# Decode attention and MLP on one core: two row blocks of one head group's query weights per layer, laid on 56 partitions and loaded from GpSimd

## The chip, the cores and the metric

The kernel runs on one core of one Trainium2 chip. The metric is the device time of one execution in microseconds. Three executions of the kernel before took 1343.22, 1343.85 and 1345.13 us; the median is 1343.85 us.

## The reference

One token of width 640 passes through attention, an MLP, the same attention again and the same MLP again, each with a residual:

```
def _A_ref(x, k_cache, v_cache, wq, wo):
    q = (x @ wq).reshape(B, Sq, H, Dh).transpose(...)
    scores = einsum("bhqd,bhkd->bhqk", q, k_cache) * (Dh ** -0.5)
    o = einsum("bhqk,bhkd->bhqd", softmax(scores), v_cache)
    return o.transpose(...).reshape(B, Sq, H * Dh) @ wo
x = x + _A_ref(_layernorm(x), k_cache, v_cache, wq, wo)
x = x + relu(_layernorm(x) @ w1) @ w2
x = x + _A_ref(_layernorm(x), k_cache, v_cache, wq, wo)
x = x + relu(_layernorm(x) @ w1) @ w2
```

There are 32 heads of width 128 and 8192 cached positions, all in float32. The keys and values of one head are 8.4 MB, and both layers read the same cache, so each layer streams some 268 MB from HBM; a few units are kept on chip between the layers. The query weights `wq` are 640 x 4096, the output weights `wo` 4096 x 640.

## The kernel before, in words

**The stream.** The host lays keys and values out as units of up to 6 MB, each with 128 rows, one for each SBUF partition. `pump` (line 179) issues the next unit on SyncE's DMA queue as soon as `place` (line 160) finds room for it in one large tile, `ring`; `release` (line 248) frees a piece when the matmuls that read it have been written out, and calls `pump` again. The tail of the same tile, `by_parts`, holds blocks of `w2`, and at the start of layer 1 two units of keys and values.

**The heads.** For each head `scores` (line 511) multiplies the keys by the query, `largest`, `exponentials` and `turn` make the probabilities, `values` (line 562) multiplies the values by them, `output` (line 582) adds the parts up. The order of the heads is fixed by `HEADS`; four heads make a group, eight groups a layer.

**The weights of a group.** The tile `both_t` has 5120 floats for each partition. Its first half, `wq_t`, holds the query weights of one group: five row blocks ("chunks", 128 rows of `wq` each) of 512 columns, one row of a block on each partition. The second half, `wo_t`, holds the output weights of a group. `load_wo` (line 276) fills both halves with a single load from the array `wqo`, in which the query weights of group k+1 lie beside the output weights of group k; it is issued on ScalarE's DMA queue (line 280, 2560 KB).

**The order of the side work.** `due` (line 778) appends small tasks to two lists, `chores` and `slow`, when a head begins, and `side_work` (line 804) takes a step of them between the pieces of a head. `run_out(k)` (line 725) multiplies the outputs of group k by `wo` and then calls `load_wo(L, k + 1, ...)`; it is due at the first head of group k+1. `queries_of(k + 1)` is due at the third head of group k; its `wide_queries` (line 435) makes the queries of a whole group by five matmuls, one for each chunk, whose partial sums lie in four strips of one PSUM bank (lines 440 and 452 to 459):

```
for c in range(NB):
    strip = c % 4
    nc.tensor.matmul(pq[32 * strip : 32 * strip + 32],
                     xc[:, c : c + 1].to_broadcast([P, 32]), wq_t[:, c], ...)
```

**GpSimd** has almost nothing to do in the kernel before: a few memsets at the start and one power (line 336, `inv_std`) for each layer norm. It issues no DMA.

Of the kernel before, what the change touches and what calls it, by code (L numbers as in the profile page):

```python
# [10 lines left out]
F32 = mybir.dt.float32  # L11
# [4 lines left out]
P = 128  # L16
D = 640
H = 32
SK = 8192
DH = 128  # L20
DFF = 1728
EPS = 1e-5
NB = D // P
HG = 4
NG = H // HG
# [58 lines left out]
GROUPS = [[heads[a] // HG for a in range(0, H, HG)] for heads in HEADS]  # L84
# [3 lines left out]
RING = 4248  # L88
WC_AT = [5, 8]
MIX_AT = [[7, 9, 11, 13], [12, 16, 20, 24]]  # L90
FLAT = 3072
EDGE = 4096
BIG = 1536
# [19 lines left out]
W2_UNITS = SLOTS * D // 8  # L113
# [10 lines left out]


@with_exitstack
def decode_kernel(ctx: ExitStack, tc: tile.TileContext, x, kv, wq, wo, wqo, w1, w2, out):
    nc = tc.nc
    consts = ctx.enter_context(tc.tile_pool(name="consts", bufs=1))
    wts = ctx.enter_context(tc.tile_pool(name="wts", bufs=1))  # L130
# [7 lines left out]

    ring = consts.tile([P, 8 * (RING + W2_UNITS)], F32, name="ring")
    by_parts = ring[:, 8 * RING :]
# [8 lines left out]
    dram_at, o = {}, 0  # L151
# [119 lines left out]
    wo_t = both_t[:, HG * D :].rearrange("p (j d) -> p j d", d=D)  # L271

    def load_wq(g, queue):
        queue.dma_start(both_t[:, : HG * D], wq[P * g : P * g + P])

    def load_wo(L, k, queue):

        g = GROUPS[L][k]
        if 0 < k < NG - 1:
            queue.dma_start(both_t, wqo[L, k - 1])  # L280
# [132 lines left out]
    def queries(g, xc, r):  # L413

        pq = side
        for c in range(NB):
            for j in range(HG):
                nc.tensor.matmul(
                    pq[32 * j : 32 * j + 32, :DH],
                    xc[:, c : c + 1].to_broadcast([P, 32]),  # L420
                    wq_t[:, c, j * DH : (j + 1) * DH],
                    start=(c == 0),
                    stop=(c == NB - 1),
                )
        yield "dve"
        row = work.tile([P, DR], F32, name="q_row")[:, :DH]
        nc.vector.tensor_scalar(row, pq[:, :DH], r[0], SCALE, op0=ALU.mult, op1=ALU.mult)
        yield "pe"
        pt = side
        nc.tensor.matmul(pt[:, :HG], row, sel[:, :HG], start=True, stop=True)  # L430
        yield "dve"
        qT[g] = work.tile([P, HG], F32, name="qT", bufs=2)
        nc.vector.tensor_copy(qT[g], pt[:, :HG])

    def wide_queries(g, xc, r):

        pq = side
        for c in range(NB):
            strip = c % 4
            nc.tensor.matmul(  # L440
                pq[32 * strip : 32 * strip + 32],
                xc[:, c : c + 1].to_broadcast([P, 32]),
                wq_t[:, c],
                start=c < 4,
                stop=c in (1, 2, 3, 4),
                skip_group_check=True,
            )
# [246 lines left out]
    def attention_and_mlp(L, xr, s, before=None):  # L694
# [25 lines left out]
                    queue.pop(0)  # L720

        def queries_of(k):
            yield from wide_queries(groups[k], xc, r)

        def run_out(k):

# [51 lines left out]
        def due(h):  # L778

            where = heads.index(h)  # L780
            k, j = divmod(where, HG)
            if j == 0:
                o_cols[k] = work.tile([P, HG], F32, name="o_cols", bufs=2)
                sums[k] = work.tile([P, HG], F32, name="sums", bufs=2) if k < NG - 1 else None
            if where and j == 0:
                chores.append([run_out(k - 1), "pe"])
            if j == 2 and k + 1 < NG:
                slow.append([queries_of(k + 1), "pe"])
            if where == H - 2:
                chores.append([first_of_last(), "pe"])  # L790
            if where == H - 1:
                chores.append([before_last(), "pe"])
            if L == 0 and where == H - HG:
                slow.append([centre_query(NG - 1, HG - 1), "pe"])
            if L == 0 and where == 4:
                nc.scalar.dma_start(w1_t, w1)
            if where == WC_AT[L]:
                nc.scalar.dma_start(wo_last, wo[last // HG][:, last % HG])
# [85 lines left out]
    def mlp(L, o, last, xp, ph):  # L884
# [128 lines left out]
        for c in range(NB):  # L1013
            g = c % 4
            nc.tensor.matmul(
                pq[32 * g : 32 * g + 32, :DH],
                cols[:, c : c + 1].to_broadcast([P, 32]),
                wq_t[:, c, (HG - 1) * DH :],
                start=c < 4,
                stop=c in (1, 2, 3, 4),  # L1020
                skip_group_check=True,
            )
# [43 lines left out]
def _laid_out(A_x, A_k_cache, A_v_cache, A_wq, A_wo, B_w1, B_w2):  # L1066
    k = np.asarray(A_k_cache)[0].reshape(H, 4, 4, RUN, DH).transpose(0, 4, 1, 2, 3)
    v = np.asarray(A_v_cache)[0].reshape(H, 4, 4, NBL, 4, 32, DH).transpose(0, 1, 5, 3, 4, 2, 6)
    v = v.reshape(H, P, NBL, 4, 4, DH)
    kv = np.empty(H * P * SK * 2, k.dtype)  # L1070
    o = 0
    for u in ORDER:
        n = 8 * size(u)
        block = kv[o : o + P * n].reshape(P, n)
        o += P * n
        a = 0
        for h, kind, piece in UNITS[u[0]][u[1]]:
# [12 lines left out]
    w2[W2_LAST:, -1, : D // 2] = w2[:W2_LAST, -1, D // 2 :]  # L1090
    wq = np.asarray(A_wq).reshape(NB, P, NG, HG * DH).transpose(2, 1, 0, 3).reshape(NG, P, HG * D)
# [5 lines left out]
    return {  # L1097
        "x": np.repeat(np.asarray(A_x).reshape(D)[_COLS].reshape(4, DR), 32, axis=0),
        "kv": kv,
        "wq": wq.reshape(NG * P, HG * D),  # L1100
        "wo": wo,
        "wqo": np.array(wqo),
        "w1": np.asarray(B_w1).reshape(NB, P, DFF).transpose(1, 0, 2),
        "w2": np.array(
            [
                np.concatenate(
                    [
                        np.concatenate([w2[:, b, : w2_width((b,))] for b in part], 1).reshape(-1)
                        for part in loads
                    ]  # L1110
                )
                for loads in W2_LOADS
            ]
        ),
    }


# [22 lines left out]
```

## Time and profile before

| | |
|---|---|
| median of three executions | 1343.85 us |
| profiled execution, span from its first to its last instruction | 1340.6 us |
| its own time: the span and what lies around it | not given apart; the median is 3.25 us above the span |
| HBM read | 570.83 MB, 426 GB/s over the span |
| busy: TensorE matmul, VectorE, ScalarE, GpSimd | 65%, 22%, 5%, 0% |
| DMA, mean busy share of 16 engines | 9 tenths or more in 39 of 40 slices |

The page gives the busy time of each engine, the span in forty slices, the DMA queues, the chain of work that ended last, the costliest groups of instructions and the DMA issues. q1 is the queue that SyncE fills, q10 that of ScalarE, q8 and q14 carry instructions. The "DMA share" of a window is the time that the packets begun in it took, as a share of 16 engines' time; 9/16 is 0.56.

### The profile page before, as it was taken

Reading aid. Unit: us, or ns where it says so; the run is one execution under the profiler, and the core shown is the slowest. Engines: PE = TensorE matmul, PEld = TensorE weight load, DVE = VectorE, ACT = ScalarE, POOL = GpSimd, SP = SyncE. Lnnn points to the kernel's source line nnn. Section 1 sums busy time; section 2 is a strip of 40 time slices with the busy share of each in tenths; the row PEclk is TensorE's granted clock in tenths of the full one; section 3 lists DMA queues with packets and bytes.
Section 4 is the critical chain, followed back from the end, with each engine's and each line's share of the span. In section 5 each row is a group of like instructions: output and inputs, shape, how many; then the busy total and the mean of one; then the engine's idle time right before and its main releaser. Section 6 shows DMA issues by size and latency. Waiting matters only on the chain.

```text
span 1340.6 us, 13403 instructions
## 1 busy us (share of the span) xinstructions
PE 874.0 (65%) x5806; PEld 255.5 (19%) x5806; DVE 290.2 (22%) x956; ACT 62.6 (5%) x155; POOL 2.9 (0%) x10
## 2 busy tenths in 40 slices
PE   5463575767657656676688755657566666567687
PEld 2110121111111111112243211112111111111123
DVE  2120121211212112223123212221221212212222
ACT  0000000000000000000000000000000000000000
POOL 0000000000000000000000000000000000000000
PEclk8686787988777887788799977887778787888789
DMA  9999999999999999999999999999999999999998
GB/s 395 431 435 430 442 423 437 429 428 437 432 434 429 428 439 426 433 425 415 425 396 425 430 435 433 432 433 431 433 429 434 432 428 433 437 427 436 425 424 333
DMA packets 24546, 571.70 MB, mean 426 GB/s; under 512 B 2724, under 2 KB 2984, under 8 KB 6952
## 3 DMA queue, kind: packets, MB, share of 16 engines
q1 hardware_dynamic: 21464, 529.31, 92.1%
q10 hardware_dynamic: 3024, 41.53, 7.3%
q8 instruction: 46, 0.75, 0.2%
q14 instruction: 12, 0.10, 0.0%
HBM read 570.83 MB, written 0.00 MB: 426 GB/s over the span
## 4 chain that ended last, share of the span: by engine, by line
DMA 67%; PE 27%; DVE 4%; ACT 1%; issue 1%; SPq 0%; ACTq 0%; DVEq 0%
DMA ring<-in_kv 66%; PE ps L516 10%; PE outs L570 9%; PE side L672 1%; DMA ring<-in_w 1%; DVE p L591 1%; PE acc L621 1%; PE side L440 1%; ACT p L545 1%; DVE h_t L531 1%; PE small L536 1%; PE small L604 1%; PE side L454 1%; DVE p L552 0%; DVE h_t L537 0%
## 5 line engine op out<-in xcount | busy, mean ns | idle before, releaser
L516 PE MATMUL ps<-ring,spread_q 128*32 128x512 f32 (+3 forms) x2088 | 332.7, 727 | 149.2 <-DMA ring<-in_kv 148.6
L570 PE MATMUL outs<-ring,p 128*4 128x512 f32 (+3 forms) x2080 | 310.6, 732 | 164.1 <-DMA ring<-in_kv 95.7
L531 DVE TENSOR_REDUCE h_t<-ps 128x1 f32<-128x512 f32 x64 | 44.3, 691 | 365.4 <-PE ps L516 365.4
L570 PEld LDWEIGHTS outs<-ring,p 128*4 128x4 f32 x2080 | 50.6, 95 | 348.4 <-issue 233.8
L516 PEld LDWEIGHTS ps<-ring,spread_q 128*32 128x32 f32 x2088 | 63.9, 124 | 277.5 <-issue 188.8
L545 ACT ACTIVATE p<-ps,h_t 128x512 f32<-128x512 f32 x63 | 43.3, 687 | 1161.2 <-DVE h_t L537 1161.2
L552 DVE STREAM_TRANSPOSE p<-p 128x128 f32<-128x128 f32 x256 | 79.8, 312 | 63.9 <-ACT p L545 57.2
L587 DVE TENSOR_SCALAR p<-outs,ind 128x128 f32<-128x128 f32 x64 | 22.5, 351 | 317.2 <-PE outs L570 317.2
L604 PE MATMUL small<-ones,p 128*128 128x1 f32 (+1 forms) x128 | 25.3, 267 | 97.4 <-DVE p L591 97.4
L591 DVE SCALAR_TENSOR_TENSOR p<-outs,ind,p 128x128 f32<-128x128 f32 x188 | 66.0, 351 | 6.7
L536 PE MATMUL small<-ident,h_t 128*128 128x128 f32 x128 | 32.7, 339 | 40.1 <-DVE h_t L531 39.9
L604 PEld LDWEIGHTS small<-ones,p 128*128 128x128 f32 x128 | 19.9, 195 | 159.7 <-DVE p L591 158.9
L672 PE MATMUL side<-w_t,wct 128*128 128x448 f32 (+1 forms) x80 | 45.3, 651 | 0.0
L452 DVE TENSOR_SCALAR q_row<-side,ln_r 128x128 f32<-128x128 f32 x56 | 19.5, 349 | 106.0 <-PE ps L516 59.0
L440 PE MATMUL side<-both_t,ln_xc 128*32 128x512 f32 x140 | 37.3, 844 | 0.0
L536 PEld LDWEIGHTS small<-ident,h_t 128*128 128x128 f32 x128 | 20.0, 196 | 89.0 <-DVE h_t L531 85.5
L621 PE MATMUL acc<-both_t,o_cols 128*64 128x320 f32 x220 | 34.6, 458 | 0.0
L454 PEld LDWEIGHTS side<-sel,q_row 128*128 128x128 f32 x112 | 19.3, 216 | 56.3 <-DVE q_row L452 29.9
L537 DVE TENSOR_REDUCE h_t<-small 128x1 f32<-128x128 f32 x64 | 18.7, 292 | 35.4 <-PE small L536 35.4
L454 PE MATMUL side<-sel,q_row 128*128 128x1 f32 x112 | 24.1, 284 | 0.3 <-DVE q_row L452 0.2
L621 PEld LDWEIGHTS acc<-both_t,o_cols 128*64 128x64 f32 x220 | 15.5, 147 | 29.4 <-issue 17.7
L672 PEld LDWEIGHTS side<-w_t,wct 128*128 128x128 f32 x80 | 13.5, 211 | 32.4 <-issue 32.4
(148 smaller groups left out, 219.5 us busy)
## 6 DMA issues: line engine op xcount, KB each, us to landing
ring<-in_kv SPq DMA_DIRECT2D x50, 6144.0 KB, 35.0
ring<-in_kv SPq DMA_DIRECT2D x23, 4096.0 KB, 33.2
ring<-in_kv SPq DMA_DIRECT2D x29, 2048.0 KB, 27.7
both_t<-in_wqo ACTq DMA_DIRECT2D x12, 2560.0 KB, 24.7
ring<-in_kv SPq DMA_DIRECT2D x4, 5120.0 KB, 34.6
ring<-in_kv SPq DMA_DIRECT2D x9, 1024.0 KB, 23.9
w_t<-in_w ACTq DMA_DIRECT2D x1, 4320.0 KB
ring<-in_kv SPq DMA_DIRECT2D x5, 768.0 KB, 29.5
```

The source lines that it names most:

```text
L440: nc.tensor.matmul(pq[32 * strip : 32 * strip + 32], xc[:, c : c + 1].to_broadcast([P, 32]), wq_t[:, c], start=c < 4, stop=c in (1, 2, 3, ...
L454: nc.tensor.matmul(mine[:, :1], row, one_of_each, start=True, stop=True, skip_group_check=True)
L516: nc.tensor.matmul(hd.ps[32 * g : 32 * g + 32, c : c + n], spread_q[:, 3 - r : 35 - r], tile_of[:, at + g * n : at + (g + 1) * n], start=f ...
L531: nc.vector.tensor_reduce(hd.nm, hd.ps, AX.X, ALU.max, negate=True)
L536: nc.tensor.matmul(pt[:, :P], hd.nm.to_broadcast([P, P]), ident, start=True, stop=True)
L545: nc.scalar.activation(hd.p, hd.ps, AF.Exp, bias=hd.low, scale=scale, accum_out=hd.l)
L552: nc.vector.transpose(hd.all_p[:, b * P : (b + 1) * P], hd.p[:, b * P : (b + 1) * P])
L570: nc.tensor.matmul((hd.out if r0 < 2 else hd.out_2)[32 * g : 32 * g + 4, r0:r1].rearrange("p r d -> p (r d)"), hd.all_p[:, 32 * i : 32 * i ...
L591: nc.vector.scalar_tensor_tensor(oc, hd.out[:, r], ind[:, r : r + 1], oc, op0=ALU.mult, op1=ALU.add)
L604: nc.tensor.matmul(pt[:, :n], part, mask.to_broadcast([P, n]), start=i == 0, stop=i == len(parts) - 1,)
L621: nc.tensor.matmul(acc[64 * g : 64 * g + 64, : 2 * DR], col.to_broadcast([P, 64]), wt[:, 2 * DR * g : 2 * DR * (g + 1)], start=first, stop ...
L672: nc.tensor.matmul(pt[:, :n], wct[:, c], w1_t[:, c, f : f + n], start=(c == 0), stop=(c == NB - 1),)
```

## The change

For the load with k = 2 of each layer (the query weights of the fourth group in order) two of the five chunks, numbers 3 and 4, leave the load on ScalarE's queue. Their 256 rows of 512 floats are laid on 56 partitions instead of 128: 44 partitions hold five rows each, 12 hold three (`held`). GpSimd loads them with 15 DMAs (`loads`), from a new array `early` in HBM: nine carry data (partitions 0 to 11, 16 to 19, 28 to 31, 96 to 99 and 92 to 95, then 32 to 43 with three slots, 48 to 51, 60 to 67 and 124 to 127), and six carry four or twelve floats a partition that nothing reads. The first number of a load is how many pieces its source is divided into where that is more than one; a load with a 1 there has three or five pieces against four partitions. The rows of a partition lie in up to five slots of 512 + 8 floats; the slots take the first two chunks' place in `both_t` and 1576 floats before it, so `both_t` is now the last part of `ring`, with 1600 more floats in front of it that were unused and are set to zero at the start. `POS` puts chunks 4 and 3 first in `wq_t`, so that the rest is one stretch.

The matmul of such a slot needs the normalized input in the order in which the rows lie. `early_columns`, due at the fifth head of each layer, makes these columns: two matmuls bring the columns of chunks 3 and 4 into a row, eight copies of VectorE put their pieces in place on a zeroed row in `mix`, five small matmuls turn the row back into five columns. `wide_queries` then uses three whole chunks and five slots for that group: eight matmuls instead of five.

```
+EARLY = {2: dict(chunks=[3, 4], slots=5,
+        held=[(5, [(0, 12), (16, 4), (28, 4), (48, 4), (60, 8), (92, 8), (124, 4)]),
+              (3, [(32, 12)])],
+        loads=[(3, 0, 12, 5), (1, 12, 4, 0), (1, 16, 4, 5), (2, 20, 8, 0),
+               (1, 28, 4, 5), (1, 96, 4, 5), (6, 68, 24, 0), (1, 92, 4, 5),
+               (3, 32, 12, 3), (1, 12, 4, 0), (1, 48, 4, 5), (2, 20, 8, 0),
+               (2, 60, 8, 5), (6, 68, 24, 0), (1, 124, 4, 5)])}
+EARLY_IN = [[2], [2]]
...
+def split(load):
+    engines, _, rows, slots = load
+    pieces = engines if engines > 1 else slots or 3
+    n = rows * (slots * HG * DH if slots else 12 if engines == 1 else 4)
+    return pieces, n // pieces
...
-    both_t = wts.tile([P, 2 * HG * D], F32, name="both_t")
+    both_t = ring[:, both_at:]
...
+    def load_early(L, k):
+        spec = EARLY[k]
+        for i, load in enumerate(spec["loads"]):
+            engines, first, rows, slots = load
+            pieces, n = split(load)
+            o = EARLY_AT[L, k, i]
+            o_end = o + pieces * (n + GAP)
+            source = early[o:o_end].rearrange("(g m) -> g m", g=pieces)[:, :n]
+            where = slots_of(spec)[first : first + rows]
+            if slots:
+                where = where[:, :slots, : HG * DH]
...
+            nc.gpsimd.dma_start(where, source)
...
         if 0 < k < NG - 1:
-            queue.dma_start(both_t, wqo[L, k - 1])
+            n = HG * DH * len(EARLY[k]["chunks"]) if k in EARLY_IN[L] else 0
+            queue.dma_start(both_t[:, n:], wqo[L, k - 1, :, n:])
+            if k in EARLY_IN[L]:
+                load_early(L, k)
             return
...
+    nc.vector.memset(ring[:, both_at - 8 * 200 : both_at], 0.0)
...
+    def early_columns(L, xc):
+        for i, c in enumerate((3, 4)):
+            nc.tensor.matmul(pt[:32, i * P : (i + 1) * P],
+                xc[:, c : c + 1].to_broadcast([P, 32]), ident, start=True, stop=True)
+        yield "dve"
+        nc.vector.memset(row, 0.0)
...
+                nc.vector.tensor_copy(row[:, a : a + slots, first : first + m], source)
...
+        yield "pe"
+        for s in range(n):
+            nc.tensor.matmul(pt[:, s : s + 1], row[:, s], sel[:32, :1], start=True, stop=True)
+        yield "dve"
+        held = work.tile([P, 8], F32, name="early_x")
+        nc.vector.tensor_copy(held[:, :n], pt[:, :n])
...
-    def wide_queries(g, xc, r):
+    def wide_queries(g, xc, r, k=None):
...
+        parts = [(xc[:, c : c + 1], wq_t[:, POS[c]]) for c in range(NB)]
+        if k in early_x:
+            spec = EARLY[k]
+            parts = [p for c, p in enumerate(parts) if c not in spec["chunks"]]
+            parts += [(early_x[k][:, s : s + 1], slots_of(spec)[:, s, : HG * DH])
+                      for s in range(spec["slots"])]
...
+            if where == 4:
+                slow.append([early_columns(L, xc), "pe"])
```

More of the change, by code (lines that the diff above doesn't have):

```diff
@@ L90, with placed, filled @@
 MIX_AT = [[7, 9, 11, 13], [12, 16, 20, 24]]
+POS = {4: 0, 3: 1, 0: 2, 1: 3, 2: 4}
+SLOT = HG * DH + 8
+GAP = 64
+EARLY = {
+    2: dict(
+        chunks=[3, 4],
+        slots=5,
+        held=[
+            (5, [(0, 12), (16, 4), (28, 4), (48, 4), (60, 8), (92, 8), (124, 4)]),
+            (3, [(32, 12)]),
+        ],
+        loads=[
+            (3, 0, 12, 5),
+            (1, 12, 4, 0),
+            (1, 16, 4, 5),
+            (2, 20, 8, 0),
+            (1, 28, 4, 5),
+            (1, 96, 4, 5),
+            (6, 68, 24, 0),
+            (1, 92, 4, 5),
+            (3, 32, 12, 3),
+            (1, 12, 4, 0),
+            (1, 48, 4, 5),
+            (2, 20, 8, 0),
+            (2, 60, 8, 5),
+            (6, 68, 24, 0),
+            (1, 124, 4, 5),
+        ],
+    ),
+}
+EARLY_IN = [[2], [2]]
+def placed(spec):
+    o = 0
+    for slots, runs in spec["held"]:
+        n = sum(m for _, m in runs)
+        for first, m in runs:
+            yield slots, first, m, o, n
+            o += m
+        o += (slots - 1) * n
+def filled(spec):
+    at = np.full((spec["slots"], P), -1)
+    for slots, first, m, o, n in placed(spec):
+        for s in range(slots):
+            for i in range(m):
+                c, d = divmod(o + s * n + i, P)
+                at[s, first + i] = P * spec["chunks"][c] + d
+    held = np.sort(at[at >= 0])
+    assert (held == np.concatenate([P * c + np.arange(P) for c in spec["chunks"]])).all()
+    loaded = np.zeros((spec["slots"], P), bool)
+    for _, first, rows, slots in spec["loads"]:
+        loaded[:slots, first : first + rows] = True
+    assert loaded[at >= 0].all()
+    return at
+def split(load):
[3 more added lines that the diff above has]
+    return pieces, n // pieces
+EARLY_AT, _o = {}, 0
+for _L in range(2):
+    for _k in EARLY_IN[_L]:
+        for _i, _load in enumerate(EARLY[_k]["loads"]):
+            EARLY_AT[_L, _k, _i] = _o
+            _pieces, _n = split(_load)
+            _o += _pieces * (_n + GAP)
+EARLY_SIZE = _o
 FLAT = 3072
@@ L126, in decode_kernel @@
 @with_exitstack
-def decode_kernel(ctx: ExitStack, tc: tile.TileContext, x, kv, wq, wo, wqo, w1, w2, out):
+def decode_kernel(ctx: ExitStack, tc: tile.TileContext, x, kv, wq, wo, wqo, w1, w2, early, out):
     nc = tc.nc
     consts = ctx.enter_context(tc.tile_pool(name="consts", bufs=1))
-    wts = ctx.enter_context(tc.tile_pool(name="wts", bufs=1))
     work = ctx.enter_context(tc.tile_pool(name="work", bufs=1))
@@ L722, in queries_of @@
         def queries_of(k):
-            yield from wide_queries(groups[k], xc, r)
+            yield from wide_queries(groups[k], xc, r, k - 1)
         def run_out(k):
@@ L1114, in _laid_out @@
         ),
+        "early": early,
     }
```

71 lines of the change are left out of this document (62 added, 9 removed).

## The prediction

> **What bounds the kernel now.** I read the page's head and queues first, then windows of time, then the chain of waits around the two places where the stream ends.
>
> ```profile
> span 1340.6 us, 13403 instructions
> PE 874.0 (65%) x5806; PEld 255.5 (19%) x5806; DVE 290.2 (22%) x956; ACT 62.6 (5%) x155; POOL 2.9 (0%) x10
> DMA packets 24546, 571.70 MB, mean 426 GB/s; under 512 B 2724, under 2 KB 2984, under 8 KB 6952
> q1 hardware_dynamic: 21464, 529.31, 92.1%
> q10 hardware_dynamic: 3024, 41.53, 7.3%
> q8 instruction: 46, 0.75, 0.2%
> DMA 67%; PE 27%; DVE 4%; ACT 1%; issue 1%; SPq 0%; ACTq 0%; DVEq 0%
> ```
>
> The queues' shares add up to 99.6% of 16 engines' span: the DMA engines hardly ever rest, and what each of them has to carry sets the end. A row on q1 moves at 529.31 MB / (0.921 x 16 x 1340.6 us) = 26.8 KB per us and engine, one on q10 at 41.53 / (0.073 x 16 x 1340.6) = 26.5. So a row of keys and values of 49,152 bytes takes 1.83 us.
>
> The share of the engines that still have something to do, in windows before the two ends of the stream (columns: window, length, busy time of five engines, granted clock, DMA share, GB/s):
>
> ```profile
> 300.00:500.00 200.00, 125.41 (x724) 32.10 (x728) 39.83 (x127) 7.51 (x19) 0.00 (x0) 0.80 1.00 432
> 634.00:639.00 5.00, 2.39 (x52) 1.09 (x43) 0.00 (x0) 0.00 (x0) 0.00 (x0) 1.00 0.93 354
> 690.00:696.00 6.00, 5.23 (x91) 4.22 (x94) 1.55 (x7) 0.74 (x3) 0.00 (x0) 1.00 0.88 335
> 1300.00:1331.00 31.00, 25.57 (x256) 10.59 (x248) 8.96 (x31) 2.30 (x7) 0.00 (x0) 1.00 1.01 421
> 1331.00:1332.70 1.70, 1.44 (x41) 1.30 (x45) 0.17 (x1) 0.00 (x0) 0.00 (x0) 1.00 0.74 300
> 1332.70:1334.70 2.00, 1.99 (x54) 1.58 (x50) 0.68 (x4) 0.00 (x0) 0.00 (x0) 1.00 0.54 221
> 1334.70:1336.40 1.70, 1.51 (x34) 0.89 (x26) 0.49 (x4) 0.00 (x0) 0.55 (x1) 1.00 0.33 120
> ```
>
> All 16 engines work until 1331.0. From 1332.7 to 1334.7 the share is 0.54, close to 9/16 = 0.56; the last engine ends at about 1336.4. So seven engines finish some 4.5 us before the last, though every load gives each the same bytes. The idle time in the last three windows is (0.26 x 1.7 + 0.46 x 2.0 + 0.67 x 1.7) x 16 = 40 us of one engine: a perfect balance would end 2.5 us sooner. In layer 0 the seven run dry at 634 to 639 and 690 to 696 (5.6 and 11.5 us of one engine). What the nine have more is probably the instruction queue: 46 packets at 0.2% of 16 x 1340.6 us, some 43 us, or 4.8 us for each of nine engines over both layers. That is an inference; no row names an engine.
>
> ```profile
> 573.46 34.55 DMA ring<-in_kv
> 622.83 17.26 DMA ring<-in_kv
> 648.54 35.72 DMA ring<-in_kv
> 1316.50 19.15 DMA ring<-in_w
> 1335.70 0.75 PE side L482 x16
> ```
>
> The chain (start, length, what) runs over such landings, and a load has landed only when the last engine has. What the nine late engines are spared before 648 and before 1316 therefore comes off the end in both layers.
>
> **The change part by part.**
>
> *The load on ScalarE's queue.* Its rows shrink from 20,480 to 16,384 bytes in one load of each layer; with 128 rows on 16 engines each engine is spared 8 x 4,096 = 32,768 bytes, at 26.5 KB/us 1.24 us a layer, 2.47 us in all.
>
> *The nine data loads.* 512 KB come back on 56 partitions, eight partitions for each of seven engines: 40 rows of 2,048 bytes on four engines, 32 on three, that is 3.09 and 2.47 us, less the 1.24 spared: +1.85 and +1.23 us. The seven early engines have about 4.5 us at 1336 and take this without becoming last: in layer 1 they would end near 1331.9 + 1.85 = 1333.8, the nine at 1335.2. That the chosen seven are the early seven rests on the number alone.
>
> *Six idle loads and fifteen completion marks.* Every one of the 15 loads may leave a mark on all 16 engines, and the idle loads give the nine a few packets of 16 bytes. No row has their price. Below: nothing. Above: as much as the nearest row with a size, the 2,560-byte row of `wo_last` (0.097 us at 26.5), 15 times a layer, 1.45 us, which would eat the gain.
>
> ```profile
> q10 hardware_dynamic: 288, 2.95, 17.0%
> wo_last<-in_wo ACTq DMA_DIRECT2D x1, 320.0 KB, 36.5
> L798 ACTq DMA_DIRECT2D wo_last<-in_wo x2: 334/334/335, 127.2 to 823.9; - x2
> ```
>
> In the 41 us from 124 to 165 q10's 288 packets, marks among them, took 0.17 x 16 x 41 = 111.5 us of one engine, and 2.95 MB at 26.5 are 111.3: small packets cost next to nothing beyond their bytes. I take 0.02 us each, 0.3 us a layer.
>
> *When the parts are there.* The rows' readers before are the queries of the group before (line 440); GpSimd waits for nothing else, while ScalarE's load waits for the output product as well. POOL's queue holds nothing behind the parts until the power at 699.17.
>
> ```profile
> 161.59 0.59 PE L440 MATMUL side<-both_t,ln_xc 128*32 128x512 f32 x1
> 205.14 0.33 ACTq L280 DMA_DIRECT2D both_t<-in_wqo  x1
> 247.64 1.45 PE L440 MATMUL side<-both_t,ln_xc 128*32 128x512 f32 x9
> 800.92 0.59 PE L440 MATMUL side<-both_t,ln_xc 128*32 128x512 f32 x1
> 846.49 0.33 ACTq L280 DMA_DIRECT2D both_t<-in_wqo  x1
> 883.90 2.37 PE L440 MATMUL side<-both_t,ln_xc 128*32 128x512 f32 x9
> 699.17 0.55 POOL L336 TENSOR_TENSOR ln_r<-ln_v,mhalf 128x1 f32<-128x1 f32 x1 [688.98 <-DVE ln_v L334]
> ```
>
> So GpSimd can start near 162 and 801.5, 85 and 82 us ahead of the need; beside ScalarE's load it would be 42.5 and 37.4. How long 40 small rows take is bounded by two readings. Below: their bytes, 3.1 us. Above: each waits for one row of keys and values, as `wo_last` shows: its 8 rows behind the 8 of line 280 landed at 127.2 + 36.5 = 163.7, 16 rows in 40.1 us since 123.66, and 16 x 1.83 plus their own 7 us are 36. By that 40 rows take 40 x (1.83 + 0.08) = 76 us, and 5 us more beside the eight rows on q10: 81 us. I take the upper reading; the parts land just in time or a few us late. That is covered: a 6 MB unit needs 14.6 us at 432 GB/s and lands 35 us after its issue, so some 20 us of work stand queued for the DMA engines while TensorE waits, and TensorE, busy 25.48 of 43 us, catches up.
>
> ```profile
> ring<-in_kv SPq DMA_DIRECT2D x50, 6144.0 KB, 35.0
> 205.00:248.00 43.00, 25.48 (x144) 6.05 (x146) 7.69 (x24) 2.09 (x5) 0.00 (x0) 0.80 1.02 439
> L323 DVE MEMSET outs<- x1: 485/485/485, 1.8 to 1.8; 128x512 f32 x1
> 6.66 0.32 DVE L1041 TENSOR_REDUCE x_s<-xr 128x1 f32<-128x160 f32 x1 [4.24 <-DMA xr<-in_x]
> ```
>
> *GpSimd's issues.* No row has one; ScalarE's takes 0.33 us, so 15 take 5 us at least. Three times as much would still be a small part of the 82 us, on an engine that is busy 2.9 us in all.
>
> *The engines' extra work.* The memset of 1600 columns is 1600/512 x 0.485 = 1.5 us, inside VectorE's wait of 4.24 us for `x`. Eight matmuls instead of five, two and five more for the columns, about ten short instructions of VectorE: by the rows of line 440 (0.59 us) and the memset at most 5 us a layer, inside the 17.5 us that TensorE is idle in each 43. Without that cover, 10 us.
>
> *Sum.* 2 x (1.24 - 0.3) = 1.9 us off: 1340.6 becomes 1338.7, and with the 3.25 us by which the median stands above this span 1343.85 becomes **1342.0**. With the costs at nothing it is 1341.4, with the upper one 1344.3.
>
> A rule of the Trainium skill speaks against this. "DMA: Bandwidth & Descriptors", section "Latency and other measured facts", says that engines 7 and 15 are usually slower than the others, and guesses that the ring of GpSimd's descriptors crowds their ports. By the partitions two of the seven are these; if they belonged to the late nine, the time would be that of rival A. GpSimd issues no DMA in this trace, and no row names an engine, so no run here shows it yet.
>
> **The rivals.**
>
> *A, the parts fall on late engines.* The list reaches its engines only if each load takes the next ones in turn. Against this rival: the numbers in the list add up to 16 twice, so the second half meets the first half's engines again. For it: nothing in the trace shows how GpSimd's loads are dealt out. If the sequence is off by some places, some of the late nine get +1.85 us in each layer instead of -1.24: 1343.85 + 2 x (1.85 + 0.3) = **1348.2**. It decides as soon as one data load falls on the last of the nine. The Trainium skill ("DMA: Bandwidth & Descriptors", "Why a DMA increments its semaphore by 16 and not by 1") has a cursor that gives GpSimd's loads the next engines in turn, and an exception that spreads some loads over all 16; by the exception this rival holds in a milder form. No run here shows either.
>
> *B, the parts come late and TensorE waits.* If GpSimd starts with ScalarE's load at 205 and 846, 81 us later is 286 and 927, 38 and 44 us after the need. TensorE stops, and behind it the scores of the next heads, their releases and SyncE's issues. After 20 us the queue of keys and values is dry, the small rows then pass at once, and the DMA engines idle until the next unit is issued, about 5 us a layer: 1343.85 + 10 - 1.9 = **1352.0**. It decides from a start later than 247.6 + 20 - 81 = 187. For it: the loads stand behind `load_wo` in the program. Against: GpSimd's queue is empty and its condition is met at 162.
>
> *C, hidden or eaten.* The marks cost the upper price, or the first stage's gain is lost in the turn between the layers: about **1343.5**. Against: the rows at 648.54 and 1316.50.
>
> *D, more than forecast.* The costs are nothing, and the seven's idle time at 634 and 690, (5.6 + 11.5) / 16 = 1.1 us of all engines, is put to use as well: 1343.85 - 2.47 - 1.1 = **1340.3**. Against: there the stream waits for TensorE's side work at 622.83 and 692, which the change doesn't shorten.
>
> **How the numbers follow.** The forecast has 0.50, A 0.13, B 0.08, C 0.19, D 0.10. Alone, the forecast's own range is 1341.2 to 1343.0. To leave out no more than 2 in 10 the range runs from 1340.6 (between D and the forecast's edge) to 1347.6 (most of A). About 0.2%, 2.7 us, is what a measurement of this kernel can tell from no change: faster means below 1341.2, slower above 1346.5. D and a fifth of the forecast, its lower edge, give 0.20; most of A and B 0.17; the rest 0.63.
>
> **What would show it.** In the changed profile a queue of GpSimd's should hold about 1 MB. Its first issue stands near 162 and 801; near 205 speaks for B, and then the matmuls of line 440's successor show a wait for a DMA at 247. Windows before the end: the share should stay above 0.9 for longer and fall from 1 to nothing in some 3 us instead of 5.4; a fall to less than 9/16 with a later end means A. The last landing of `w2` should come about 1.9 us sooner. The forecast is wrong if the span is above 1341 or below 1337.5.

## The result, and the profile after

The changed kernel takes 1386.63 us in the median (1384.57 to 1388.09); the kernel before, on the same chip, 1343.96. The ratio is 1.0318, with a 95% interval of 1.0304 to 1.0333: some 43 us slower, where 1342.0 us were forecast. The profiled execution spans 1382.6 us against 1340.6.

The head of the changed kernel's page, its queues (packets, MB, share of 16 engines' span) and the shares of the chain that ended last:

```profile
span 1382.6 us, 13573 instructions
DMA packets 27970, 571.73 MB, mean 414 GB/s; under 512 B 5892, under 2 KB 6152, under 8 KB 10376
q1 hardware_dynamic: 21464, 529.31, 89.6%
q10 hardware_dynamic: 3024, 40.49, 6.9%
q0 software_dynamic: 3424, 1.08, 0.3%
q8 instruction: 46, 0.75, 0.2%
DMA 49%; PE 26%; issue 17%; DVE 4%; POOL 1%; ACT 1%; another core or an unknown queue 1%; SPq 0%; ACTq 0%; POOLq 0%; DVEq 0%
```

The queues' shares now add up to 97.0% instead of 99.6%. In time of all 16 engines that is 1341.1 us busy and 41.5 idle, against 1335.2 and 5.4 before. So of the 42.0 us that the span grew, about 36 are idle time of the DMA engines and about 6 are busy time, though the bytes are the same (571.73 and 571.70 MB). Each share is rounded to 0.1%, so the 6 is good to some 1.5 us. In the chain 17% is now "issue", which was 1%. q0 is GpSimd's queue, and it holds 3,424 packets where 15 loads of each layer carry 1.08 MB. Packets under 512 bytes went from 2,724 to 5,892: 3,168 of the 3,424 are tiny.

Where the idle time lies is seen in TensorE's waits (in all, times, longest) and in TensorE's timeline at the two places (start, length, instruction, idle time before it and what ended that):

```profile
PE side L591 <- DMA ring<-in_early: 57.7, 2, 29.3
```

```profile
279.51 2.74 PE L591 MATMUL side<-ring,early_x 128*32 128x512 f32 x9 [29.26 <-DMA ring<-in_early]
...
937.41 2.74 PE L591 MATMUL side<-ring,early_x 128*32 128x512 f32 x9 [28.43 <-DMA ring<-in_early]
```

These are the matmuls of line 440's successor, which now read the five slots. They were due where the row of before has 247.64 and 883.90; TensorE stands for 29.3 and 28.4 us until the parts are there.

GpSimd's issues in layer 0:

```profile
163.12 2.90 POOL L370 DMA_DIRECT2D ring<-in_early  x4 [152.37 <-PE ps L667]
187.74 0.72 POOL L370 DMA_DIRECT2D ring<-in_early  x1 [21.71 <-issue]
209.93 1.30 POOL L370 DMA_DIRECT2D ring<-in_early  x2 [21.47 <-issue]
234.43 1.42 POOL L370 DMA_DIRECT2D ring<-in_early  x2 [23.20 <-issue]
249.77 0.66 POOL L370 DMA_DIRECT2D ring<-in_early  x1 [13.92 <-issue]
270.63 2.60 POOL L370 DMA_DIRECT2D ring<-in_early  x4 [20.20 <-issue]
275.04 0.72 POOL L370 DMA_DIRECT2D ring<-in_early  x1 [1.81 <-issue]
```

It starts at 163.12, where the prediction put it, 85 us ahead of the need. But after four loads it stops, and goes on one or two loads at a time, some 14 to 23 us apart; the last of the 15 leaves it at 275.04. These gaps, 199 us in both layers, are most of the chain's "issue".

What the engines did with the two queues is counted in windows. Three windows of the changed kernel: from 190 to 204, from 164 to 249, and from 268 to 279 (q1 carries keys and values, q0 GpSimd's loads):

```profile
q1 hardware_dynamic: 139, 6.05, 100.7%
q0 software_dynamic: 139, 0.03, 1.1%
```

```profile
q1 hardware_dynamic: 816, 33.74, 92.7%
q10 hardware_dynamic: 146, 2.10, 5.8%
q0 software_dynamic: 776, 0.25, 1.2%
```

```profile
q0 software_dynamic: 745, 0.24, 10.4%
q1 hardware_dynamic: 23, 0.34, 7.3%
```

While keys and values are queued, one packet of q0 passes for each row of q1: 139 and 139. In the 85 us up to the need, 776 of q0's packets passed, 48.5 on each engine, 1.75 us apart. That isn't even half of the layer's 1,712. When SyncE's queue had run dry at 268, 745 passed within 11 us.

The windows of the changed kernel around the stalls (window, length, busy time of five engines, granted clock, DMA share, GB/s):

```profile
250.00:268.00 18.00, 0.25 (x3) 0.00 (x0) 0.00 (x0) 0.00 (x0) 0.43 (x1) 0.50 1.03 437
268.00:279.00 11.00, 0.00 (x0) 0.00 (x0) 0.00 (x0) 0.00 (x0) 3.33 (x5) 0.50 0.18 53
279.00:291.00 12.00, 9.39 (x51) 2.70 (x51) 3.60 (x11) 0.78 (x2) 0.00 (x0) 0.78 0.00 1
291.00:294.00 3.00, 3.00 (x22) 0.93 (x26) 0.16 (x1) 0.00 (x0) 0.00 (x0) 0.77 0.85 262
920.00:927.00 7.00, 0.00 (x0) 0.00 (x0) 0.00 (x0) 0.00 (x0) 0.00 (x0) 0.50 0.91 389
927.00:938.00 11.00, 0.59 (x4) 0.23 (x8) 0.00 (x0) 0.00 (x0) 3.34 (x5) 0.50 0.10 21
938.00:949.00 11.00, 8.90 (x51) 2.48 (x43) 3.60 (x11) 0.78 (x2) 0.00 (x0) 0.81 0.60 225
```

From 250 to 268 TensorE already stands, but the DMA engines are full: that is the queued work which the prediction counted as cover. Then they idle: 0.82 x 11 + 12 + 0.15 x 3 = 21.5 us in layer 0, and 0.09 x 7 + 0.90 x 11 + 0.40 x 11 = 14.9 us in layer 1, together 36.4, which is the 36 of the queues' shares. The second part of each stall comes after the parts have landed: SyncE may only issue when TensorE has worked off a unit, and that takes from 279.5 to 291.0 in layer 0.

```profile
291.01 8.90 SPq L265 DMA_DIRECT2D ring<-in_kv  x2
```

(That is the first unit issued since 245.4; in layer 1 it follows at 941.9, 4.5 us after TensorE has gone on.)

### The profile page after: what moved, and what is told of

The parts are those of the page before. It is cut to its first block, busy times and chain, and to the rows that moved or that the text cites. A ratio compares the mean times of both kernels' runs of the same rounds, so it can differ in the third digit from the quotient of the medians.

```text
span 1382.6 us, 13573 instructions
## 1 busy us (share of the span) xinstructions
PE 886.6 (64%) x5846; PEld 260.3 (19%) x5846; DVE 294.8 (21%) x977; ACT 62.6 (5%) x155; POOL 23.5 (2%) x40
## 2 busy tenths in 40 slices
DMA packets 27970, 571.73 MB, mean 414 GB/s; under 512 B 5892, under 2 KB 6152, under 8 KB 10376
## 3 DMA queue, kind: packets, MB, share of 16 engines
q0 software_dynamic: 3424, 1.08, 0.3%
## 4 chain that ended last, share of the span: by engine, by line
DMA 49%; PE 26%; issue 17%; DVE 4%; POOL 1%; ACT 1%; another core or an unknown queue 1%; SPq 0%; ACTq 0%; POOLq 0%; DVEq 0%
DMA ring<-in_kv 46%; PE ps L667 10%; PE outs L721 9%; DMA ring<-in_w 2%; PE side L591 2%; DMA ring<-in_wqo 1%; POOL ring L370 1%; DVE p L742 1%; DVE h_t L682 1%; ACT p L696 1%; PE small L687 1%; PE acc L772 1%; PE side L823 1%; PE side L605 1%
## 5 line engine op out<-in xcount | busy, mean ns | idle before, releaser
L721 PE MATMUL outs<-ring,p 128*4 128x512 f32 (+3 forms) x2080 | 324.7, 762 | 157.6 <-DMA ring<-in_kv 86.0
L667 PE MATMUL ps<-ring,spread_q 128*32 128x512 f32 (+3 forms) x2104 | 329.0, 714 | 125.8 <-DMA ring<-in_kv 125.2
L591 PE MATMUL side<-ring,early_x 128*32 128x512 f32 x20 | 6.8, 1037 | 57.7 <-DMA ring<-in_early 57.7
L591 PE MATMUL side<-ring,ln_xc 128*32 128x512 f32 x132 | 33.9, 832 | 0.0
L772 PE MATMUL acc<-ring,o_cols 128*64 128x320 f32 x220 | 32.9, 441 | 0.0
L370 POOL DMA_DIRECT2D ring<-in_early x30 | 20.5, 687 | 447.1 <-PE ps L667 247.8
```

The costliest lines, as they stand in the source:

```text
L591: nc.tensor.matmul(pq[32 * strip : 32 * strip + 32], column.to_broadcast([P, 32]), weights, start=c < 4, stop=c >= len(parts) - 4, skip_gr ...
L667: nc.tensor.matmul(hd.ps[32 * g : 32 * g + 32, c : c + n], spread_q[:, 3 - r : 35 - r], tile_of[:, at + g * n : at + (g + 1) * n], start=f ...
L721: nc.tensor.matmul((hd.out if r0 < 2 else hd.out_2)[32 * g : 32 * g + 4, r0:r1].rearrange("p r d -> p (r d)"), hd.all_p[:, 32 * i : 32 * i ...
L772: nc.tensor.matmul(acc[64 * g : 64 * g + 64, : 2 * DR], col.to_broadcast([P, 64]), wt[:, 2 * DR * g : 2 * DR * (g + 1)], start=first, stop ...
```

## The experiments

The theory after the result: **packets, not bytes and not lateness**. Every one of GpSimd's loads puts packets on all 16 engines, and on the engines that carry none of its data as many tiny ones as it has data packets on the loaded ones. In the trace two rows of 2,048 bytes make one packet of 4,096. So eight data loads give 10 packets on every engine, the one with three slots 6, the six idle loads one each, and each of the 15 one completion mark: 8 x 10 + 6 + 6 + 15 = 107 on every engine, 1,712 in a layer, 3,424 in all, as the page has it. No row names an engine; that every engine has the same number is read from these counts and from the turns that q0 takes with q1, whose rows go to all 16. One after the other, at a row of keys and values each, they need 107 x 1.83 = 196 us, and there are 85. The page bears the count out from another side: 2 x 128 packets of data leave 3,168 tiny ones, the growth seen above. The rivals: GpSimd's queue is slow whatever it carries; GpSimd starts too late (the condition of the prediction's rival B); it can hold only four loads, some 20 us each; the parts are on the wrong engines (rival A); the side work costs.

**Nobody loads the two chunks.** The kernel before, whose load on ScalarE's queue leaves two chunks of that group out in both layers (0 and 1, which lie first in this kernel); the queries of that group come from old weights. It measures what the whole change could win at best.

```
-            queue.dma_start(both_t, wqo[L, k - 1])
+            n = 2 * HG * DH if k == 2 else 0
+            queue.dma_start(both_t[:, n:], wqo[L, k - 1, :, n:])
```

> The kernel before, with chunks 0 and 1 of the query weights left out of ScalarE's load with k = 2 in each layer and loaded by nobody, so the queries of that group use old weights (that part of the computation is wrong). It measures by itself the term that the prediction put at 2.47 us: every DMA engine is spared 32 KB a layer. Theory of the balance (the last engine sets the end): 2.0 to 2.8 us faster than before. Rival (hidden at the turn of the layers): 0 to 1.3 us faster.

Measured: 1341.51 us (1340.46 to 1344.9), a ratio of 0.9991 [0.9982, 1.0000], span 1339.7. All 16 engines are spared the bytes here, and the gain is 1.7 us in the median and 0.9 in the span, with 0 and 2.4 as its bounds. This lies between the two ranges that were expected. So no placing of these bytes could have won more than some 2.4 us.

**One load of GpSimd's with 128 rows.** The same, and GpSimd brings these two chunks as one load of 128 rows of 4,096 bytes.

```
+            if n:
+                nc.gpsimd.dma_start(both_t[:, :n], wqo[L, k - 1, :, :n])
```

> The kernel before, with the same two chunks of the load k = 2 taken over by one GpSimd load of 128 rows of 4,096 bytes; the computation is whole. Theory of the rounds (each packet of GpSimd's queue waits for one row of keys and values on its engine, 1.83 us): 8 packets and a mark on each engine, in place about 17 us after the start near 162, no wait of TensorE for it, time within 1 us of before. Rival (a GpSimd load as such delays the stream, by its issue or its descriptors): some 5 us or more slower.

Measured: 1343.47 us, ratio 1.0001 [0.9992, 1.0010]. The timeline of GpSimd and the page's row of its queue:

```profile
162.00 0.70 POOL L283 DMA_DIRECT2D both_t<-in_wqo  x1 [151.78 <-PE side L443]
...
801.39 0.57 POOL L283 DMA_DIRECT2D both_t<-in_wqo  x1 [94.72 <-PE side L443]
```

```profile
q0 software_dynamic: 288, 1.05, 0.2%
```

The same megabyte on the same queue at the same times passes in 9 packets on each engine and layer, and nothing waits for it. The queue as such isn't slow. What differs is 9 packets against 107.

**The new loads in layer 0 alone.** Layer 1 loads and computes as before.

```
-EARLY_IN = [[2], [2]]
+EARLY_IN = [[2], []]
```

> The changed kernel with the new loads in layer 0 alone; layer 1 loads and computes as before. If each layer's stall is its own, the span is about 20 to 22 us above that of before, half of the changed kernel's 42, with a wait of TensorE for the new loads of about 29 us, once.

Measured: 1367.19 us in a single execution, 24 us above the kernel before, span 1365.4. One wait of TensorE for `early` is left, of 32.2 us; both are a little more than expected. The two layers' losses are separate and add up: 24 us here leave 19 for layer 1, and the idle times of the two layers were 21.5 and 14.9.

**Eight loads of three slots.** Only the first half of the list; of the two chunks only these parts are loaded, the rest of the slots holds old data.

```
-            (3, 0, 12, 5),
+            (3, 0, 12, 3),
...
-            (3, 32, 12, 3),
... (and the six loads behind it)
```

> The changed kernel with only the first eight of its 15 loads and three slots instead of five in each (the other rows are not loaded, so the queries of that group are wrong). Theory of the rounds: five loads of 6 packets, three idle loads of one, eight marks make 41 packets on each of the 16 engines, 656 a layer and 1,312 in all; 41 x 1.83 = 75 us, in place near 238 and 877, before the need at 247 and 884, so TensorE has no wait for them worth the name and the time is 1 to 3 us below before. Rival (GpSimd has room for four loads and then waits 20 us for each further pair, whatever they hold): the loads are issued at the same distances as in the changed kernel, the eighth after 230. Rival (the extra matmuls and copies cost the time): still some 20 us or more slower than before.

Measured: 1344.67 us, ratio 1.0013 [1.0005, 1.0022], no wait for the parts, and exactly the 1,312 packets that the theory counts. The gain of 1 to 3 us that was expected did not come. And these three slots lie wholly ahead of the weights' tile, so GpSimd was free to load them from 10.63 on: it says nothing on lateness, and the next run repeats it with a late start.

**The same eight loads, not before the group before is done.** The three slots are now the last three, which lie on the weights that the group before reads; again only these parts are loaded.

```
-                where = where[:, :slots, : HG * DH]
+                where = where[:, 5 - slots :, : HG * DH]
```

> The shortened list of the third experiment (five loads of three slots, three idle ones; the rest of those weights is not loaded, so the queries of that group are wrong), now in slots 2 to 4, which overlap the weights of the group before, so that GpSimd starts near 162 and 801 as in the changed kernel and not at 11. Theory of the rounds: 41 packets on each engine at 1.83 us, last landing near 238 and 877, no wait of TensorE for them, time as in the third experiment (1342 to 1346). Rival (whatever GpSimd starts at 162 comes too late, by its room for four loads): a wait of 10 us or more at 248, slower than before by 5 us or more.

Measured: 1343.73 us, ratio 1.0006 [0.9994, 1.0018], no wait for the parts. GpSimd's issues, and the two queues in the window from 167 to 242:

```profile
166.31 3.40 POOL L362 DMA_DIRECT2D ring<-in_early  x5 [155.50 <-PE ps L659]
183.17 1.26 POOL L362 DMA_DIRECT2D ring<-in_early  x2 [13.46 <-issue]
186.44 0.66 POOL L362 DMA_DIRECT2D ring<-in_early  x1 [2.01 <-issue]
```

```profile
q1 hardware_dynamic: 701, 29.88, 93.0%
q0 software_dynamic: 656, 0.18, 1.0%
```

GpSimd starts 3 us later than in the changed kernel and is through in time. All 656 packets of the layer, 41 on each engine, lie in this window, and a window from 170.4 to 241.9 holds all of them too: 71.5 us, 1.74 us each, close to the 1.83 that the prediction took for a row of keys and values. Five loads leave at once and the next two after 13.5 us, so "four loads, 20 us each" isn't the rule either. A start at 166 is early enough for 41 packets and not for 107: the count decides.

**The changed kernel without the six idle loads.** This takes 12 packets off each engine in a layer.

```
-            (1, 12, 4, 0),
-            (2, 20, 8, 0),
-            (6, 68, 24, 0),
... (each of them twice)
```

> The changed kernel without its six idle loads, so the nine data loads take whatever engines come next; the computation is whole. Theory of the rounds: eight loads of 10 packets, one of 6 and nine marks make 95 packets on each engine and layer (3,040 in all) instead of 107; 95 x 1.83 = 174 us are still more than the 85 available plus the 20 that the queue covers, so TensorE still waits 25 to 30 us in each layer and the time is 1382 to 1387. Rival (the idle loads, or the four engines they serve in between, make the delay): the wait falls by more than half.

Measured: 1381.96 us in a single execution, with a wait of 55.0 us in two places, and 3,040 packets in the whole run, 95 on each engine and layer as counted.

So the loads that carry nothing are a small part of it; by the counts the tiny packets that go with the data are the larger one. Nor is it the number of loads: nine of them with 95 packets stall almost as long as fifteen with 107, and the eight above with 41 don't stall.

**The eight loads turned by ten engines.** The list of three slots again, with an idle load over ten engines ahead and one over six behind; the data are loaded as far as there.

```
+            (10, 68, 20, 0),
             (3, 0, 12, 3),
...
+            (6, 68, 24, 0),
```

> The third experiment's kernel with an idle load of ten pieces ahead of the list and one of six behind it (again wrong queries in that group). If the loads take the engines in turn, the five data loads now fall on engines 10, 11, 12, 14, 1, 2 and 9 instead of 0, 1, 2, 4, 7, 8 and 15: five of the late nine carry about 1 us more in each layer. Then the engines end further apart, the share of busy engines falls over some 6 us before the end instead of 4, and the time is 1 to 2.5 us above the third experiment's. If the loads are dealt out without regard to order, both stay as they are.

Measured: 1345.99 us, ratio 1.0017 [1.0008, 1.0026], against 1.0013 without the turn: the times don't tell the two apart. The ends of the stream differ, in one profile each. First the eight loads as listed, then turned, then once more as listed, but with the late start:

```profile
1331.00:1332.70 1.70, 1.70 (x55) 1.40 (x44) 0.00 (x0) 0.00 (x0) 0.00 (x0) 1.00 0.77 310
1332.70:1334.70 2.00, 1.99 (x44) 1.59 (x40) 1.02 (x6) 0.00 (x0) 0.00 (x0) 1.00 0.54 214
1334.70:1336.40 1.70, 1.65 (x34) 0.75 (x33) 0.16 (x1) 0.00 (x0) 0.56 (x1) 1.00 0.12 44
```

```profile
1335.00:1337.00 2.00, 2.00 (x61) 1.67 (x53) 0.00 (x0) 0.00 (x0) 0.00 (x0) 1.00 0.61 252
1337.00:1339.00 2.00, 1.80 (x33) 1.35 (x36) 1.18 (x7) 0.00 (x0) 0.00 (x0) 1.00 0.45 174
1339.00:1340.50 1.50, 1.46 (x32) 0.58 (x26) 0.00 (x0) 0.00 (x0) 0.56 (x1) 1.00 0.06 20
```

```profile
1336.50:1338.20 1.70, 1.70 (x55) 1.39 (x44) 0.00 (x0) 0.00 (x0) 0.00 (x0) 1.00 0.64 262
1338.20:1340.20 2.00, 1.87 (x38) 1.41 (x36) 1.10 (x7) 0.00 (x0) 0.00 (x0) 1.00 0.42 163
1340.20:1341.90 1.70, 1.54 (x32) 0.72 (x32) 0.09 (x1) 0.00 (x0) 0.56 (x1) 1.00 0.09 35
```

Each packet can be paired with the one that ended just before it began; by this estimate the engines' last packets end about 4 us apart as listed, 5.7 turned, and about 6 when nobody loads the chunks. That fits parts that fall on early engines as listed and on others when turned. But the late run has the list untouched, and there they end 5.4 us apart, close to the turned one. Its engines ran partly dry between the layers (see the next run), so that less of layer 0's parts may count at the end. The order is made likely by this and not shown.

**The side work alone.** The changed kernel without its 15 loads; the slots hold old data.

```
-            if k in EARLY_IN[L]:
-                load_early(L, k)
```

> The changed kernel without any of GpSimd's 15 loads (the two chunks are not loaded, so the queries of that group are wrong); the extra matmuls, copies and the zeroing stay. If that work is hidden, the time is that of the first experiment, 1340.5 to 1342.5. Rival (the side work or the new place of the tile costs what the third experiment showed above the first): 1343.5 to 1345.5.

Measured: 1343.26 us (1340.46 to 1347.75), ratio 0.9998 [0.9986, 1.0010], span 1339.7, which is the span without side work and without these bytes. That is between the two ranges that were expected. The times lie in two groups, 1340.5 to 1343.8 and 1345.8 to 1347.8, and the profile is of the lower one. The runs of three slots have such groups too, and the profile of the one with the late start (1347.24 us) is of the upper one. There the granted clock is 0.50 for 5 us between the layers, where it is 1.00 in this run's profile, and the DMA engines run partly dry (0.91 here, 0.82 in the 10 us behind it):

```profile
705.00:710.00 5.00, 5.00 (x30) 2.75 (x34) 1.03 (x7) 0.00 (x0) 0.00 (x0) 0.50 0.91 377
```

Whether that is what divides the groups one profile can't tell. A cost of the side work of 1 or 2 us can't be excluded; the 43 us are not in it.

**One chunk, in time.** Chunk 4 alone, in three slots ahead of the weights' tile, so that GpSimd can load it long before its need. The list has 12 loads, seven with data and five idle.

```
-        chunks=[3, 4], slots=5,
+        chunks=[4], slots=3,
...
-        end = both_at + HG * DH * len(spec["chunks"])
+        end = both_at
```

> A whole computation without the stall: one chunk of the load with k = 2 in each layer, in three slots in front of the weights' tile, loaded by GpSimd a group or more ahead. 7 data loads of 6 packets, 4 idle ones and 11 marks make 57 packets on each engine and layer. Theory (each packet of GpSimd's queue costs every engine some 0.02 us, and sparing 16 KB gives 0.4 to 0.6 us a layer): 114 x 0.02 = 2.3 us lost, 0.8 to 1.2 gained, 1 to 2 us slower than before, no wait for the new loads. Rival (the balance pays once the stall is gone): 0.5 to 1.5 us faster.

Measured: 1344.39 us, ratio 1.0010 [1.0001, 1.0019], no wait for the parts. q0 holds 1,888 packets, 59 on each engine and layer: 7 x 6 with data or beside it, 5 idle ones and 12 marks. The expectation had left one idle load and its mark out of the count. With the wait gone the change still doesn't pay: 0.1 to 2.6 us slower.

**One chunk for three groups of each layer.** The same for k = 2, 4 and 6, to multiply what a packet costs. In layer 0 the turn between the layers reads the chunk of the last of these at its old place, so part of the last group's queries come from old weights.

```
-EARLY_IN = [[2], [2]]
+EARLY = {2: LOW, 4: HIGH, 6: LOW}
+EARLY_IN = [[2, 4, 6], [2, 4, 6]]
```

> A whole computation that starts the parts early: one chunk instead of two, in three slots that all lie in front of the weights' tile, so that GpSimd can load them one to two groups ahead, and this for k = 2, 4 and 6 of each layer. Theory of the rounds: 57 to 59 packets a load list, 104 us, in place well ahead, no wait of TensorE; the nine late engines are spared 3 x 0.62 us a layer. If small packets cost next to nothing: 1.5 to 3.5 us faster than before. Rival (each of some 345 packets of GpSimd's queue costs every engine 0.04 us, as the third experiment stands above the first by 3.2 us with 82): 8 to 12 us slower than before.

Measured: 1348.86 us, ratio 1.0044 [1.0026, 1.0061], 5,952 packets on q0, 372 on each engine, and no wait for the parts. Two windows with GpSimd's packets, then the same two of the kernel before:

```profile
255.00:350.00 95.00, 66.99 (x362) 16.84 (x362) 18.68 (x61) 4.51 (x12) 5.73 (x9) 0.80 1.00 426
...
425.00:520.00 95.00, 58.87 (x344) 15.32 (x344) 19.59 (x64) 3.90 (x10) 4.49 (x7) 0.77 1.00 426
```

```profile
255.00:350.00 95.00, 64.61 (x362) 16.28 (x362) 18.68 (x61) 4.62 (x12) 0.00 (x0) 0.84 1.00 432
...
425.00:520.00 95.00, 59.42 (x360) 15.46 (x360) 20.24 (x66) 3.42 (x10) 0.00 (x0) 0.82 1.00 431
```

The engines are full in both, but move 426 GB/s instead of 431 to 432: 1.3% of 95 us, 1.2 us for the 59 to 68 packets that each engine passes in such a stretch, about 0.02 us a packet. The end of the stream in this kernel:

```profile
1338.00:1340.00 2.00, 1.99 (x56) 1.59 (x48) 0.37 (x3) 0.00 (x0) 0.00 (x0) 1.00 1.01 398
1340.00:1342.00 2.00, 1.78 (x42) 1.22 (x34) 0.81 (x5) 0.00 (x0) 0.48 (x1) 1.00 0.36 137
```

All engines work until 1340, and after 1342 the share is 0.00: they end within some 2 us of each other, where it was 5.4 before. It is 5.4 us slower all the same, between the two ranges that were expected: 372 x 0.02 = 7.4 us of packets, less what the balance brings.

## Why the prediction was wrong, point by point

**"When the parts are there" failed, in the count.** Its price was right: one row of keys and values for a packet (139 and 139; 41 packets in 71.5 us, 1.74 us each). Its start was right: 163.12 for "near 162". In layer 1 it was 826.50 for 801.5, which is layer 0's loss of 24 us handed on; the need moved with it, to 909. What failed is "40 rows", the rows of the busiest engine. The packets of a load stand on all engines, those without data included; the rows pair up, so an engine's own data would be 16 to 20 packets, but it passes 107, because the loads' packets follow one another on every engine. The working bounded the price of a small row from both sides and never bounded their number; it then called the rest covered, so the sum has no term for a stall.

Two rules of the Trainium skill bear on it. "DMA: Bandwidth & Descriptors", section "Why a DMA increments its semaphore by 16 and not by 1", has all 16 engines post a mark for each of GpSimd's loads, whatever its shape. The trace agrees: 480 packets of 4 bytes, 2 x 15 x 16. The prediction counted these marks as a cost and not in the wait. The Trainium skill's section "Queues, rings and completion order" on the same page has each engine take the queues in turn, packet by packet; 139 against 139 agrees.

**Rival B came true, with a wrong reason, size and marker.** Its place (the fourth group's queries, in both layers) and its chain (TensorE, the units' release, SyncE's issue, idle DMA engines) are what the trace shows. Its condition, a start later than 187, was not met, and the marker named for it, a first issue near 205, spoke against it while it happened. The cover of "some 20 us" was right: the engines stayed full from 250 to 268. "About 5 us a layer" of idle time was 21.5 and 14.9, for two causes that it left out. "The small rows then pass at once" held for what had been issued; but GpSimd still had five loads to issue, from 270.63 to 275.04, and the last took 4.2 us more to land:

```profile
275.04 4.23 DMA ring<-in_early
...
279.51 2.74 PE side L591 x9
```

(These are rows of the chain of waits of the changed kernel.) And the first unit's release came 4.5 to 11.5 us after TensorE went on, not at once.

**"Six idle loads and fifteen completion marks" had the right price and the wrong number.** 0.02 us each is what three groups measured, though no row had given the prediction more than its bounds, nothing and 0.097 us, so that the match is luck; but there are 107 in a layer, not 15, so 2.1 us instead of 0.3, above the upper bound of 1.45. In the changed kernel itself the engines are busy 5.9 us longer for the same bytes, 0.028 us for each of 214 packets.

**"The load on ScalarE's queue" was oversized as a gain.** q10 did get shorter by 97.9 - 95.4 = 2.5 us of all engines, as worked out. But the end moved by only 1.7 us when these bytes were left out altogether (0 to 2.4). By 0.02 us each the packets cost 2 x 2.1 = 4.3 us, more than that, so without the stalls the change would lose too; one chunk in time, 1.1 us slower, shows it on a smaller scale.

**What held, and what stays open.** Seven engines do finish early: paired as above, the packets of the kernel before end by 1332.2 on seven engines and from 1334.3 on the other nine. That the list reaches early ones is likely (the ends of the run as listed and of the three groups), but not shown; in the changed kernel itself nothing can tell, so rival A is not refuted. By the cursor of the Trainium skill ("DMA: Bandwidth & Descriptors", section "Why a DMA increments its semaphore by 16 and not by 1") a turn of the list by ten places must move the parts; the ends about 4 and 5.7 us apart agree with it, the 5.4 of the late run do not clearly. The exception by which some loads spread over all 16 did not occur here: the 12 partitions of the first load, spread over 12 engines, would make three packets on each, and the count of 107 needs ten. That engines 7 and 15 are slow no run here could show, as no row names an engine. The memset, the columns and the three more matmuls stayed hidden, as far as 1 or 2 us can be told. In the changed kernel the balance came to nothing in any case: both stalls let all 16 engines run dry, so the early seven start again level with the others at 291 and 949. That is read off the windows and was not tried by itself.

The same level start speaks against the prediction's reason for the late nine, the instruction queue over both layers. From 941 to 1379, with all engines level at the start, the changed kernel's q8 has 15 packets:

```profile
q8 instruction: 15, 0.25, 0.2%
```

They took some 16 us, 1.8 us for each of nine engines. But at the end the engines are as far out of step as before:

```profile
1374.70:1376.70 2.00, 1.96 (x54) 1.46 (x42) 0.97 (x6) 0.00 (x0) 0.00 (x0) 1.00 0.50 196
```

The shares before and behind this window are 0.82 and 0.14 (1.7 us each), which makes 44 us of idle time of one engine, where the prediction worked out 40. What makes the nine late stays open.

**The sum now.** 1340.6, plus 36.4 of idle engines, plus 5.9 of longer busy time, is 1382.9; the profile has 1382.6.

Open are why GpSimd's loads fill up the engines that have nothing to carry, what sets the 14 to 23 us between its issues (5 loads leave at once in one run, 4 in another), and how much shorter the stall would be if all 15 had been issued by 268. A whole kernel of two chunks whose need comes later, at the same 107 packets, wasn't tried.

## What to carry to other kernels

Price a load by the packets that it puts on each engine's queue, idle engines and marks included, times the row of the queue with which it takes turns; bytes and rows of the busiest engine say little. Where a full queue with 48 KB rows stands beside it, every packet costs some 1.75 us of latency, so one load over 128 partitions (9 packets) arrives where fifteen small ones (107) do not. And before spending anything on a balance, leave the work out altogether: here that alone showed 1.7 us to be won, 2.4 at most.

## What the hardware showed unasked

- A GpSimd load that has data for one engine and 10 packets there puts 10 packets on each of the other 15 too, by the counts of every kernel here that has such loads. In a layer 128 packets carry 4,096 bytes each, 1,248 carry 8 bytes, 240 are marks of 4 bytes; the rest are the idle loads'.
- A tiny packet that takes its turn between 49,152-byte rows costs 0.02 to 0.03 us of its engine, of which 0.009 us is the time of the packet itself in the trace.
- GpSimd's issue takes 0.57 to 0.89 us each, 0.71 in the median of the changed kernel's 30 (2.90 us for four), about twice ScalarE's 0.33.
